# Linear attention and two MLPs on one core: kv products in halves of the array's columns, four units' q exponentials by ScalarE, v queued ahead of the first weights

## Chip, cores and metric

The kernel runs on one core of a Trainium2 chip. The metric is device time in microseconds of one execution; smaller is better. Engines are named as the profile names them: PE (TensorE matmul), PEld (TensorE weight load), DVE (VectorE), ACT (ScalarE), POOL (GpSimd) and SP (SyncE, which here only issues DMAs).

## The reference

```python
# q, k, v: 8 batches x 8 heads x 576 tokens x 64, float32
q_s = softmax(q, over the 64 features)
k_s = softmax(k, over the 576 tokens)
kv  = einsum('bhsd,bhse->bhde', k_s, v)      # 64 x 64 for each head
y   = einsum('bhsd,bhde->bhse', q_s, kv)     # -> 4608 tokens x 512
h   = y @ w_in1;  y = leaky_relu(h, 0.01) @ w_out1       # 512 -> 2048 -> 512
h   = y @ w_in2;  y = silu(h) @ w_out2                   # 512 -> 2048 -> 512
```

The softmaxes subtract the maximum and divide by the sum plus 1e-9.

## The kernel before

**Units.** Attention is cut into 36 units. Unit n is a block j of 512 output tokens (9 blocks) and a pair p of heads (4 pairs), so units 0 to 3 are block 0, units 4 to 7 are block 1, and so on. For n below 32 a unit also makes the kv of one batch and one pair of heads, so there are 32 kv products. Three generators make a unit: `k_task` (softmax of k and the kv product), `v_task` (loads of v) and `q_task` (softmax of q, transposes, and the product with kv that gives x, the operand of the first MLP layer).

**The kv product (L507 to L509).** The 576 tokens are four chunks of 128 and a rest of 64. The stationary operand is a chunk of exp(k), 128 tokens by 128 features of two heads. The moving operand is v of both heads with a column of ones behind it, 129 columns, so that the last column of the result is the sum of the softmax. The fifth matmul takes the 64 tokens of the rest, and so 64 rows of the array. Only the two diagonal 64 x 64 blocks of the result are kept: L515 and L516 make the reciprocal of the sum on DVE, and L521 copies the two blocks, scaled, into `kv` on ACT. All of it is float32, and the trace shows each float32 matmul as two instructions.

**The softmax of q (L571 to L603).** DVE takes the negated maximum (L572). For units below `NS` = 8 the maximum is subtracted in one instruction (L577), ACT takes one exponential of 512 columns (L581), and DVE sums it (L583). For later units ACT takes eight exponentials of 64 columns, each with the maximum as its bias and with a sum of its own (L592). Then DVE adds the epsilon and inverts (L598, L599), and L601 multiplies.

**The order of work.** A small planner, `Queues`, runs when the program is built. Every generator yields its next operation with an estimated cost (`op(("A", 0.4))` for ACT, `"D"` for a DMA of SP, `"p"` and `"P"` for PE), and the planner emits the one that can start first on the estimated clock. Among those that could start together the smaller rank goes first. The emitted order is the program order of each engine, and SP's order is the order of all DMAs. In `v_task` each of the three loads is planned only when the one before it has landed by the estimate. At n below 4 the ranks are r = -40 + 5n for k, r + 1 for q, r + 5 for v; the weights of the first layer (`split1(f)`, L350) have rank -36 + 6f for f below 4.

**The rest.** The first layer (`layer0`, L651 to L653) multiplies x by w_in1 as three float32r products. Its weights are decoded by DVE and ACT (`decode`, L329 to L346, then L296 and L292). It runs blocks 0 and 1 in parts, f below 6 first, and attention of the later blocks runs in between. The other three layers (L872, L922) follow, with a Strassen-like scheme on seven products. L691 stores the activations of the first layer to DRAM.

Of the kernel before, what the change touches and what calls it, by code (L numbers as in the profile page):

```python
# [13 lines left out]
ACTF = mybir.ActivationFunctionType  # L14
# [48 lines left out]
class Queues:  # L63
# [14 lines left out]
    def spawn(self, rank, gen):  # L78
        self.tasks.append([rank, next(self.count), self.now, gen, None, 0.0, None])
        self.tasks.sort(key=lambda t: t[:2])  # L80
        self.step(next(t for t in self.tasks if t[3] is gen), None)
# [121 lines left out]
def linear_attention_two_mlps(  # L203
# [24 lines left out]
    nc = tc.nc  # L228
    B, H, S, D = q.shape
    NT, DM = out.shape  # L230
    DFF = w_in1.shape[1]
    P = 128
    TB = 512
    NB = NT // TB
    NP = H // 2
# [3 lines left out]
    SR = S - SM  # L239
    EPS = 1e-9  # L240
    FS = 6
    NU = 8
    NS = 8
# [18 lines left out]
    gd = [tc.dram_tile([NG, 4, P, TB], F32, name=f"gd{j}") for j in range(NB)]  # L262

    NKV = 8
    NV = 2 * D + 1
    ident = const.tile([P, P], F32, name="ident")
    ones = const.tile([P, 1], F32, name="ones")
    kvbuf = [const.tile([P, P], F32, name=f"kv{i}") for i in range(NKV)]
# [7 lines left out]
    done, spawn = qs.done, qs.spawn  # L276
# [158 lines left out]
    sets = []  # L435
# [5 lines left out]
    for n in range(3):  # L441
        t = gp.tile([P, 2, TB], F32, tag=f"g{n}", name=f"uq{n}")
        r_q.add(t[:, 0], t[:, 1])

    def k_task(n):

        b, j, p = units[n]
        if n >= NU:
            yield wait(("kvs", n - NU))
        of[n] = yield get(r_kv)  # L450
        kf, vv = of[n]
        done(("set", n))
        heads = slice(2 * p, 2 * p + 2)

        yield op(("D", 0.73))
        nc.sync.dma_start(
            out=kf[:, 0:512].rearrange("p (h c) -> p h c", h=2),
            in_=k[b, heads, 0:SM, :].rearrange("h (p c) d -> p h (c d)", c=4),
        )
        kh = kf[:, 0:512].rearrange("p (h c d) -> p h c d", c=4, h=2)  # L460
        k4 = kf[:, 0:512].rearrange("p (h c d) -> p c h d", c=4, h=2)
        yield op(("D", 0.56))
        k1 = kf[0:SR, 512:640]
        nc.sync.dma_start(
            out=k1.rearrange("p (h d) -> p h d", h=2), in_=k[b, heads, SM:S, :].rearrange("h p d -> p h d")
        )
        m1 = yield get(r_m)
        m2 = yield get(r_o)
        m2v = m2[:, 0:4 * D].rearrange("p (h c d) -> p h c d", h=2, c=2)
        yield op(("V", v_tt(256)))  # L470
        nc.vector.tensor_tensor(out=m2v, in0=kh[:, :, 0:2], in1=kh[:, :, 2:4], op=ALU.max)
        yield op(("V", v_tt(128)))
        nc.vector.tensor_tensor(out=m1, in0=m2v[:, :, 0], in1=m2v[:, :, 1], op=ALU.max)
        r_o.put(m2)
        m1f = m1.rearrange("p h d -> p (h d)")
        yield op(("V", v_tt(128)))
        nc.vector.tensor_tensor(out=m1f[0:SR], in0=m1f[0:SR], in1=k1, op=ALU.max)
        pm = yield get(r_attn)
        yield op(("p", 0.12))
        nc.tensor.transpose(pm[:, 0:P], m1f, ident)  # L480
        r_m.put(m1)
        nm = small[n % NU]["k"][:, 0:1]
        yield op(("V", v_tt(128)))
        nc.vector.tensor_reduce(out=nm, in_=pm[:, 0:P], axis=AX.X, op=ALU.max, negate=True)
        yield op(("p", 0.12))
        nc.tensor.transpose(pm[:, P:2 * P], nm.to_broadcast([P, P]), ident)
        nb = pm[:, P:2 * P]
        yield op(("V", v_tt(512)))
        nc.vector.tensor_tensor(
            out=k4, in0=k4,  # L490
            in1=nb.rearrange("p (h d) -> p h d", h=2).unsqueeze(1).to_broadcast([P, 4, 2, D]), op=ALU.add,
        )
        yield op(("V", v_tt(128)))
        nc.vector.tensor_tensor(out=k1, in0=k1, in1=nb[0:SR], op=ALU.add)
        r_attn.put(pm)
        kx = yield get(r_kx)
        yield op(("A", a_(512)))
        nc.scalar.activation(
            out=kx.rearrange("p (c h d) -> p c h d", c=4, h=2), in_=k4, func=ACTF.Exp
        )  # L500
        yield op(("A", a_(128)))
        nc.scalar.activation(out=k1, in_=k1, func=ACTF.Exp)
        yield wait(("v", n), *([("xm", n - NKV + NP)] if n >= NKV - NP else []))
        vv = vv.rearrange("p (c n) -> p c n", c=5)
        pk = yield get(r_attn)
        yield op(("p", 1.1))
        for c in range(4):  # L507
            nc.tensor.matmul(pk[:, 0:NV], lhsT=kx[:, c * P:(c + 1) * P], rhs=vv[:, c, :], start=c == 0, stop=False)  # L508
        nc.tensor.matmul(pk[:, 0:NV], lhsT=k1, rhs=vv[0:SR, 4, :], start=False, stop=True)  # L509
        r_kv.put(of.pop(n))  # L510
        r_kx.put(kx)
        done(("kv", n))
        rk = small[n % NU]["k"][:, 1:2]
        yield op(("V", 0.15))
        nc.vector.tensor_scalar_add(rk, pk[:, 2 * D:NV], EPS)  # L515
        nc.vector.reciprocal(out=rk, in_=rk)  # L516
        w = kvbuf[(b * NP + p) % NKV]
        for i in range(2):
            o = slice(i * D, (i + 1) * D)
            yield op(("A", a_(64)))  # L520
            nc.scalar.activation(out=w[o, o], in_=pk[o, o], func=ACTF.Copy, scale=rk[o])  # L521
        kv[b, p] = w
        r_attn.put(pk)
        done(("kvs", n))

    def v_task(n):
        b, j, p = units[n]
        yield wait(("set", n))
        t = of[n][1]
        t = t.rearrange("p (c n) -> p c n", c=5)  # L530
        for i in range(2):
            yield op(("D", 0.73))
            nc.sync.dma_start(
                out=t[:, 0:4, i * D:(i + 1) * D],
                in_=v[b, 2 * p + i, 0:SM, :].rearrange("(p c) d -> p c d", c=4),
            )

            yield wait()
        yield op(("D", 0.56))
        nc.sync.dma_start(  # L540
            out=t[0:SR, 4, 0:2 * D].rearrange("p (h d) -> p h d", h=2),
            in_=v[b, 2 * p:2 * p + 2, SM:S, :].rearrange("h p d -> p h d"),
        )
        yield wait()
        done(("v", n))
# [9 lines left out]
    def q_task(n):  # L555

        b, j, p = units[n]
# [14 lines left out]
        nc.vector.tensor_reduce(out=nq, in_=qv, axis=AX.X, op=ALU.max, negate=True)  # L572
        sq = rq = small[n % NU]["rq"]
        x4 = qx.rearrange("p (c h d) -> p c h d", c=4, h=2)
        if n < NS:
            e = yield op(("G", 1.0), ("V", v_tt(512)))
            engines[e].tensor_tensor(  # L577
                out=qv, in0=qv, in1=nq.unsqueeze(2).to_broadcast([P, 8, D]), op=ALU.add
            )
            yield op(("A", a_(512)))  # L580
            nc.scalar.activation(out=x4, in_=q4, func=ACTF.Exp)  # L581
            yield op(("V", v_tt(512)))
            nc.vector.tensor_reduce(  # L583
                out=sq, in_=qx.rearrange("p (a d) -> p a d", a=8), axis=AX.X, op=ALU.add
            )
        else:

            for c in range(4):
                for h in range(2):
                    at, to = 4 * h + c, 2 * c + h  # L590
                    yield op(("A", 0.4))
                    nc.scalar.activation(  # L592
                        out=x4[:, c, h], in_=q4[:, c, h], func=ACTF.Exp, bias=nq[:, at:at + 1],
                        accum_out=sq[:, to:to + 1],
                    )
# [379 lines left out]
    with tc.manual_schedule():  # L975
        nc.vector.memset(ones, 1.0)
        make_identity(nc, ident)
        nc.scalar.activation(out=small[0]["k"][:, 0:1], in_=ones, func=ACTF.Exp)
        for _, t in sets:
            nc.gpsimd.memset(t.rearrange("p (c n) -> p c n", c=5)[:, :, 2 * D:], 1.0)  # L980
        for t in kvbuf:
            nc.gpsimd.memset(t, 0.0)

        for n in range(NP):
            r = -40 + 5 * n
            spawn(r, k_task(n))
            spawn(r + 1, q_task(n))
            spawn(r + 5, v_task(n))
        for n in range(NP, len(units)):
            b, j, p = units[n]  # L990
            r = -12 + 3 * p if j == 1 else step(j, 0) - 14 + 4 * p
            if b is not None:
                spawn(r, k_task(n))
                spawn(r, v_task(n))
            spawn(r, q_task(n))
        for f in range(NF):
            spawn(-36 + 6 * f if f < 4 else step(0, f) - 4, split1(f))
            if f < NH:
                spawn(f, layer0(0, f))
        spawn(0, layer0_all())  # L1000
        for t in (convert1, convert2, convert3):
            spawn(1000, t())
        spawn(0, later())
        for i in range(NG):
            for l in (1, 2, 3):
                spawn(step2(l, 0, i) - 8, weights(l, i))
        spawn(step2(1, 0, 0) - 4, g_all(1))
        spawn(step2(2, 0, 0) - 5, x_all())
        spawn(step2(3, 0, 0) - 4, g_all(3))
        spawn(step2(1, 0, 0), layers())  # L1010
        qs.run()
# [30 lines left out]
```

## Time and profile before

| | us |
|---|---|
| median of 3 runs (1629.92 to 1631.63) | 1631.16 |
| the profiled execution | 1635.08 |
| its span, first to last instruction | 1633.1 |
| PE busy | 1603.1 |
| DVE busy | 1194.2 |
| ACT busy | 851.3 |
| POOL busy | 39.1 |

PE is busy in 98% of the span. Busy PE is not PE at its peak: instructions overlap, so what a matmul costs is read from the distance between starts and not from its duration. Times on the left of a timeline row are microseconds from the start of the span.

### The profile page before, as it was taken

Reading aid. Unit: us, or ns where it says so; the run is one execution under the profiler, and the core shown is the slowest. Engines: PE = TensorE matmul, PEld = TensorE weight load, DVE = VectorE, ACT = ScalarE, POOL = GpSimd, SP = SyncE. Lnnn points to the kernel's source line nnn. Section 1 sums busy time; section 2 is a strip of 40 time slices with the busy share of each in tenths; the row PEclk is TensorE's granted clock in tenths of the full one; section 3 lists DMA queues with packets and bytes.
Section 4 is the critical chain, followed back from the end, with each engine's and each line's share of the span. In section 5 each row is a group of like instructions: output and inputs, shape, how many; then the busy total and the mean of one; then the engine's idle time right before and its main releaser. Section 6 shows DMA issues by size and latency. Waiting matters only on the chain.

```text
span 1633.1 us, 30896 instructions
## 1 busy us (share of the span) xinstructions
PE 1603.1 (98%) x11456; PEld 1501.8 (92%) x11456; DVE 1194.2 (73%) x2205; ACT 851.3 (52%) x1824; POOL 39.1 (2%) x53
## 2 busy tenths in 40 slices
PE   6899999999999999999999999999999999999999
PEld 4688888888788999999999999999999999999999
DVE  8886656657566887777788966666669877777775
ACT  5768756766445544444447433444446544444442
POOL 2101001000000000000000000000000000000000
PEclk9899999999999999999999999999999999999999
DMA  8766767777779655454558344333338544444442
GB/s 227 234 195 167 209 196 240 212 242 230 225 235 311 214 150 168 141 170 145 166 143 277 131 152 140 131 133 133 135 130 279 163 131 135 133 130 136 134 132 78
DMA packets 251030, 287.25 MB, mean 176 GB/s; under 512 B 59392, under 2 KB 182272, under 8 KB 250880
## 3 DMA queue, kind: packets, MB, share of 16 engines
q1 hardware_dynamic: 250880, 285.29, 56.6%
q8 instruction: 90, 1.47, 0.4%
q14 instruction: 60, 0.49, 0.1%
HBM read 168.82 MB, written 116.39 MB: 175 GB/s over the span
## 4 chain that ended last, share of the span: by engine, by line
PE 93%; DVE 5%; DMA 1%; issue 0%; ACT 0%; SPq 0%; DVEq 0%; ACTq 0%
PE b L922 22%; PE h L922 21%; PE b L872 11%; PE h L872 11%; PE h L651 8%; PE h L653 8%; PE h L652 8%; PE a L623 2%; PE a L508 2%; PE a L608 1%; DVE o L810 1%; PE a L509 1%; DVE a L292 1%; DVE x L292 1%; DVE g L292 0%
## 5 line engine op out<-in xcount | busy, mean ns | idle before, releaser
L651 PE MATMUL h<-x,w 128*128 128x512 f32 x576 | 238.5, 414 | 2.3 <-ACT w L296 1.6
L296 ACT ACTIVATE x<-x 128x512 fp32r<-128x512 f32 x209 | 131.8, 631 | 205.8 <-DMA x<-gda 91.0
L653 PE MATMUL h<-x,w 128*128 128x512 f32 x576 | 225.9, 392 | 1.2 <-DVE w L292 1.2
L652 PE MATMUL h<-x,w 128*128 128x512 f32 x576 | 225.4, 391 | 0.8 <-DVE x L292 0.5
L810 DVE TENSOR_TENSOR o<-o,b 128x512 f32<-128x512 f32 x190 | 128.1, 685 | 72.5 <-PE b L872 39.7
L810 DVE TENSOR_TENSOR o<-o,h 128x512 f32<-128x512 f32 x188 | 126.6, 685 | 62.7 <-PE h L872 36.7
L884 ACT ACTIVATE o<-o 128x512 f32<-128x512 f32 x144 | 89.2, 629 | 145.5 <-DVE o L810 144.7
L684 ACT ACTIVATE o<-h 128x512 f32<-128x512 f32 x144 | 85.9, 597 | 118.0 <-PE h L653 109.0
L296 ACT ACTIVATE x<-o 128x512 fp32r<-128x512 f32 x169 | 105.2, 631 | 70.0 <-DVE o L810 53.8
L922 PE MATMUL b<-a,x 128*128 128x256 f32 x1080 | 141.4, 283 | 0.1
L292 DVE TENSOR_TENSOR x<-x 128x512 fp32r<-128x512 f32 x209 | 137.2, 684 | 2.5
L651 PEld LDWEIGHTS h<-x,w 128*128 128x128 f32 x576 | 108.8, 189 | 29.2 <-ACT w L296 2.5
L922 PEld LDWEIGHTS b<-a,x 128*128 128x128 f32 x1080 | 134.7, 192 | 0.3 <-DVE x L292 0.3
L922 PE MATMUL b<-x,a 128*128 128x256 f32 x1044 | 132.0, 284 | 0.6 <-DVE x L292 0.5
L653 PEld LDWEIGHTS h<-x,w 128*128 128x128 f32 x576 | 108.4, 188 | 25.6 <-DVE w L292 2.3
L872 PE MATMUL h<-x,a 128*128 128x256 f32 x1008 | 130.0, 283 | 1.3 <-DVE x L292 1.3
L652 PEld LDWEIGHTS h<-x,w 128*128 128x128 f32 x576 | 108.9, 189 | 22.8 <-issue 1.2
L922 PEld LDWEIGHTS b<-x,a 128*128 128x128 f32 x1044 | 128.1, 192 | 1.1 <-DVE x L292 1.0
L872 PEld LDWEIGHTS h<-x,a 128*128 128x128 f32 x1008 | 124.9, 192 | 1.5 <-DVE x L292 1.5
L922 PE MATMUL h<-x,a 128*128 128x256 f32 x996 | 126.0, 283 | 0.2
L872 PE MATMUL b<-x,a 128*128 128x256 f32 x960 | 123.8, 283 | 1.3 <-DVE x L292 1.3
L922 PEld LDWEIGHTS h<-x,a 128*128 128x128 f32 x996 | 122.3, 192 | 0.7 <-DVE x L292 0.6
(116 smaller groups left out, 2819.3 us busy)
## 6 DMA issues: line engine op xcount, KB each, us to landing
gda<-o SPq DMA_DIRECT2D x144, 256.0 KB, 2.6
gd<-o SPq DMA_DIRECT2D x144, 256.0 KB, 2.6
x<-gd SPq DMA_DIRECT2D x102, 256.0 KB, 2.7
x<-gda SPq DMA_DIRECT2D x89, 256.0 KB, 2.8
a<-wc SPq DMA_DIRECT2D x84, 256.0 KB, 4.3
wc<-o SPq DMA_DIRECT2D x72, 256.0 KB, 3.2
raw<-in_moe_w_out_dram SPq DMA_DIRECT2D x32, 512.0 KB, 4.2
g<-gda SPq DMA_DIRECT2D x37, 256.0 KB, 2.7
```

Of the source, the lines that this page charges most:

```text
L292: engines[e].tensor_tensor(out=out_, in0=a, in1=b.bitcast(F32), op=ALU.subtract)
L296: nc.scalar.activation(out=out_, in_=in_, func=ACTF.Copy)
L508: nc.tensor.matmul(pk[:, 0:NV], lhsT=kx[:, c * P:(c + 1) * P], rhs=vv[:, c, :], start=c == 0, stop=False)
L623: nc.tensor.matmul(po, lhsT=kv[bb, p], rhs=qT.rearrange("p (c t) -> p c t", c=4)[:, :, a:e], start=True, stop=True)
L651: nc.tensor.matmul(h, lhsT=w[:, 0, kk], rhs=x[:, 0], start=kk == 0, stop=False)
L652: nc.tensor.matmul(h, lhsT=w[:, 0, kk], rhs=x[:, 1], start=False, stop=False)
L653: nc.tensor.matmul(h, lhsT=w[:, 1, kk], rhs=x[:, 0], start=False, stop=kk == KD - 1)
L684: nc.scalar.activation(out=o, in_=h, func=ACTF.Prelu, alpha=0.01)
L810: nc.vector.tensor_tensor(out=o, in0=a, in1=b, op=alu)
L872: nc.tensor.matmul(bank[:, r * HB:(r + 1) * HB], lhsT=w4[:, a, r, k], rhs=x3[:, b, k], start=n == 0, stop=n == 5,)
L884: nc.scalar.activation(out=t, in_=t, func=ACTF.Silu)
L922: nc.tensor.matmul(bank[:, m * HB:(m + 1) * HB], lhsT=s[:, a, at:at + P], rhs=x[:, b, r * HB:(r + 1) * HB], start=i + m + n == 0, stop=i = ...
```

## The change

The kv product is made per head. For each of five chunks and each of two heads one matmul has as stationary operand the chunk's 64 columns of that head, as moving operand the head's 64 columns of v with a column of ones behind them (65 columns), and writes its half of the partitions of the result. The rest of 64 tokens is now a chunk of 128 like the others, whose lower half is zeros in k and in v; POOL writes the zeros and the ones once, at the start, into the six sets of buffers. For units 0 to 3 the softmax of q takes the branch with eight exponentials. The rank of `v_task` for these units becomes r + 2.

```diff
-    NV = 2 * D + 1
+    NV = 2 * (D + 1)
...
-        for c in range(4):
-            nc.tensor.matmul(pk[:, 0:NV], lhsT=kx[:, c * P:(c + 1) * P], rhs=vv[:, c, :], start=c == 0, stop=False)
-        nc.tensor.matmul(pk[:, 0:NV], lhsT=k1, rhs=vv[0:SR, 4, :], start=False, stop=True)
+
+        for c in range(5):
+            kc = kx[:, c * P:(c + 1) * P] if c < 4 else kf[:, 512:640]
+            for h in range(2):
+                o = slice(h * D, (h + 1) * D)
+                nc.tensor.matmul(
+                    pk[o, 0:D + 1], lhsT=kc[:, o], rhs=vv[:, c, h * (D + 1):(h + 1) * (D + 1)],
+                    start=c == 0, stop=c == 4,
+                )
...
-        nc.vector.tensor_scalar_add(rk, pk[:, 2 * D:NV], EPS)
+        nc.vector.tensor_scalar_add(rk, pk[:, D:D + 1], EPS)
...
-            nc.scalar.activation(out=w[o, o], in_=pk[o, o], func=ACTF.Copy, scale=rk[o])
+            nc.scalar.activation(out=w[o, o], in_=pk[o, 0:D], func=ACTF.Copy, scale=rk[o])
...
-                out=t[:, 0:4, i * D:(i + 1) * D],
+                out=t[:, 0:4, i * (D + 1):i * (D + 1) + D],
...
-            out=t[0:SR, 4, 0:2 * D].rearrange("p (h d) -> p h d", h=2),
+            out=t[0:SR, 4].rearrange("p (h d) -> p h d", h=2)[:, :, 0:D],
...
-        if n < NS:
+        if NP <= n < NS:
...
-        for _, t in sets:
-            nc.gpsimd.memset(t.rearrange("p (c n) -> p c n", c=5)[:, :, 2 * D:], 1.0)
+        for t_, t in sets:
+            t5 = t.rearrange("p (c h d) -> p c h d", c=5, h=2)
+            nc.gpsimd.memset(t5[:, :, :, D:], 1.0)
+
+            nc.gpsimd.memset(t_[SR:P, 512:640], 0.0)
+            nc.gpsimd.memset(t5[SR:P, 4, :, 0:D], 0.0)
...
-            spawn(r + 5, v_task(n))
+            spawn(r + 2, v_task(n))
```

## Rows read from the trace of the kernel before

**Rows 1.** Windows, all engines: busy us (instructions), PEclk, DMA share, GB/s.

```profile
12.00:24.00 12.00, 8.54 (x30) 6.49 (x29) 10.56 (x23) 7.31 (x14) 3.12 (x3) 1.00 0.93 262
24.00:36.00 12.00, 10.13 (x48) 6.75 (x48) 11.45 (x27) 7.08 (x16) 3.40 (x3) 1.00 0.74 197
46.00:68.00 22.00, 17.93 (x79) 12.27 (x77) 17.86 (x51) 16.63 (x39) 6.47 (x6) 0.78 0.93 290
110.00:361.00 251.00, 251.00 (x1255) 205.89 (x1254) 160.38 (x434) 178.85 (x620) 15.88 (x15) 1.00 0.69 208
```

**Rows 2.** Timeline of PE around one kv product: start us, us, instruction.

```profile
111.48 0.39 PE L653 MATMUL h<-x,w 128*128 128x512 f32 x1
111.71 1.05 PE L508 MATMUL a<-u,kx 128*128 128x129 f32 x8
...
112.70 0.49 PE L509 MATMUL a<-u,u 64*128 64x129 f32 x2
113.11 0.50 PE L651 MATMUL h<-x,w 128*128 128x512 f32 x1
113.45 0.39 PE L652 MATMUL h<-x,w 128*128 128x512 f32 x1
```

**Rows 3.** The same stretch: the last L508 alone, then a weight load (PEld).

```profile
112.49 0.27 PE L508 MATMUL a<-u,kx 128*128 128x129 f32 x1
...
113.11 0.19 PEld L651 LDWEIGHTS h<-x,w 128*128 128x128 f32 x1
```

**Rows 4.** Windows of line L508 alone: PE busy (instructions), PEld busy.

```profile
110.00:365.00 255.00, 25.45 (x192) 24.14 (x192) 1.00 0.69 208
```

**Rows 5.** Timeline of DVE and POOL: the softmax of q of unit 1.

```profile
12.88 0.67 DVE L572 TENSOR_REDUCE q<-uq 128x8 f32<-128x512 f32 x1
...
13.63 1.04 POOL L577 TENSOR_TENSOR uq<-uq,q 128x512 f32<-128x512 f32 x1 [2.80 <-DVE q L572]
...
16.98 0.17 DVE L598 TENSOR_SCALAR rq<-rq 128x8 f32<-128x8 f32 x1
```

**Rows 6.** Timeline of DVE: the sum of unit 3, and what follows it back to back.

```profile
32.66 0.67 DVE L583 TENSOR_REDUCE rq<-o 128x8 f32<-128x512 f32 x1
33.25 0.67 DVE L292 TENSOR_TENSOR x<-a,x 128x512 fp32r<-128x512 f32 x1
```

**Rows 7.** Timeline of ACT: one exponential of 512, then exponentials of 64 with sums.

```profile
22.98 0.61 ACT L296 ACTIVATE w<-o 128x512 fp32r<-128x512 f32 x1
23.50 0.61 ACT L581 ACTIVATE o<-uq 128x512 f32<-128x512 f32 x1
...
104.32 0.34 ACT L592 ACTIVATE o<-uq,q 128x64 f32<-128x64 f32 x1
104.65 0.34 ACT L592 ACTIVATE o<-uq,q 128x64 f32<-128x64 f32 x1
```

**Rows 8.** Timeline of SP and POOL at the start, and PE's first kv product.

```profile
1.44 1.19 POOL L982 MEMSET kv<- 128x128 f32 x8
...
2.64 0.47 SPq L319 DMA_DIRECT2D rw<-in_moe_w_in_dram  x1
3.15 0.58 SPq L533 DMA_DIRECT2D u<-in_v_dram  x1
...
9.79 1.04 POOL L601 TENSOR_TENSOR o<-o,rq 128x512 f32<-128x512 f32 x1 [2.84 <-DVE rq L599]
...
10.97 0.62 SPq L540 DMA_DIRECT2D u<-in_v_dram  x1
...
14.08 1.93 PE L508 MATMUL a<-u,kx 128*128 128x129 f32 x8
```

**Rows 9.** The chain that ended last, a kv product in it: start us, us, what.

```profile
52.30 1.83 PE a L508 x8
54.13 0.73 PE a L509 x2
...
67.43 0.64 ACT w L296
```

## The prediction

> **What bounds the kernel now.** I read the page first: PE is busy in 98% of the span and holds nearly all of the chain that ended last, so the end moves only with what PE must do and with the time in which it has nothing to do. The windows by stage [rows 1] then split the span in two. From 110 to 361 us, where the attention of the later blocks runs between matmuls of the first layer, PE is busy in 251.00 of 251 us, DVE in 160 and ACT in 179. There the engines that feed PE have room, and a microsecond that PE saves is a microsecond of the end. Before 68 us PE waits. DVE is busy in 10.56 of 12 us and in 11.45 of 12 us, the DMA engines at 0.93 in the first of these windows, ACT in only 7.3 and 7.1. From 46 to 68 us PE's clock is at 0.78 on average, and the first matmul of the steady stretch starts only behind the decoded weights that ACT writes at 67.43 [rows 9]. There the end moves with DVE, SP's order and ACT. The change touches both: its kv part works on the first stretch, its q and v parts on the second.
>
> **What one kv product costs PE now.** The timeline of PE is read by starts [rows 2, 3]. The eight instructions of L508 start between 111.71 and 112.49, so 0.78 / 7 = 0.111 us apart, and the two of L509 should follow at that pace: ten times 0.111 is 1.11 us. But L509 starts at 112.70 where 112.60 was due, 0.10 late. The L652 behind the product starts at 113.45. An undisturbed matmul of the first layer takes 0.23 (L653 at 111.48, the next start at 111.71), so the product ended in effect at 113.45 - 0.23 = 113.22, which is 0.30 behind 112.70 + 2 x 0.111 = 112.92. The product costs 1.51 us: 1.11 of streaming, 0.40 for entering and leaving the 64-row shape. The weight load of the L651 behind it starts at 113.11, with its matmul and not ahead of it, which is part of those 0.30.
>
> **What it costs after.** Five chunks by two heads by two instructions make 20 instructions of 65 columns in place of 10 of 129. The 64-row shape is gone, but the array is now entered and left in halves of its columns. The trace holds no such shape. I take the same 0.40, as the nearest change of shape; the bounds are 0 (no price) and 0.80 (twice). The streaming is the open term. Half as many columns is 0.0555 us for an instruction, if it goes with the columns. If the two halves then run wholly beside each other, the 20 take 10 x 0.0555 = 0.56 us. If they don't, 20 x 0.0555 = 1.11, as now. If an instruction does not get shorter at all (bounded by its weight load or its issue), 20 x 0.111 = 2.22. The row that it is nearest to is L508, whose pitch holds a load and a matmul at once: the loads do run under matmuls here, PEld is busy in 206 of the 251 us in which PE is never idle [rows 1], and nothing in it speaks for a half-width load as long as a whole one. Between whole overlap and none I take the middle, 0.83 us: twice as many instructions must pass the same sequencer, so I do not expect the whole factor. The product then costs 0.83 + 0.40 = 1.23, which saves 0.28 us.
>
> The count: L508 has 192 instructions from 110 us on [rows 4], so 24 of the 32 products stand where PE is the bound. 24 x 0.28 = 6.7 us saved; 24 x 0.55 = 13.2 with whole overlap, 0 with none, and 24 x 1.11 = 26.6 lost at the other end. The other eight stand where PE waits anyway. Of these, one on the chain runs at the 1.2 GHz level (1.83 us for 8 is 0.229 each, twice 0.111) and takes 2.56 [rows 9]. Scaled by 1.23 / 1.51 it saves 0.5.
>
> The Trainium skill speaks against overlap at one place: "TensorE: Matmul & The Clock Gate", Part 3, says that a weight load overlaps a running matmul only when the row group differs, and the two column halves have the same rows. By it the loads of the 20 instructions would stand between the matmuls, and the product would lengthen towards the 2.22 above. The trace already disagrees for the whole array, whose loads share all rows and still hide [rows 1], so I give that case little. "TensorEngine Tiling (Array Packing)", Key Properties, says the opposite, that tiles load and multiply in parallel; no run before shows it.
>
> **q of units 0 to 3.** Three instructions change. POOL loses L577, 1.04 us a unit [rows 5]; POOL is idle most of the time, so only the latency counts. DVE loses L583, which holds it 0.59 (starts at 32.66 and 33.25) [rows 6]: 4 x 0.59 = 2.4 us. ACT loses one exponential of 0.52 (22.98 to 23.50 is the pitch of such instructions) and gains eight of 0.33 (104.32 to 104.65, with the read of the accumulator inside) [rows 7]: 2.64 - 0.52 = 2.1 us a unit, 8.5 in all. ACT was busy in 14.4 of the 24 us from 12 to 36 [rows 1]; with three units' share there, 6.4, it is at 20.8 of 24: full, but not the bound. The path itself gets no longer: from the maximum to the epsilon takes 16.98 - 12.88 = 4.1 us now, through three engines [rows 5], and eight exponentials after a maximum of 0.67 are 3.3. What queues behind the eight on ACT are the exponentials of k and the copies that x needs; a copy that comes late by up to 0.33 holds up its x. DVE was nearly full from 12 to 36 us, and the weights that PE waits for at 68 us are decoded on it, so I take DVE's 2.4 us as gained. Bounds: 4 lost (ACT's 8.5 less what its 9.6 idle us in these windows can't take at the right time, about half) and 4 gained (DVE's 2.4, and PE's clock not falling).
>
> **v, and the fills.** By the ranks, v of unit 0 passes the first weights and nothing else: unit 1's v already stood ahead of unit 2's k by the order in which they are spawned, and the others stay behind the same loads. SP issues the weights at 2.64 and the first piece of v at 3.15 [rows 8]; they swap, so v is 0.5 earlier and the weights 0.6 later. PE's first kv product starts at 14.08, 3.1 us behind the issue of the last piece of v at 10.97, so it may come up to 1.5 earlier by the planned chain of three loads; the first decode comes 0.6 later. I take 0, bounds 1.5 gained and 0.6 lost. The ones and zeros are 18 fills in place of 6. By the 1.19 / 8 = 0.15 of the fills of kv, 12 more are 1.8 us, and POOL is done at 2.63 + 1.8 = 4.4. Its next work now is L601 at about 9.8 [rows 8], so they cost nothing; if a load of k had to wait for them it would cost under 1 us.
>
> **Sum.** Against the profiled execution, 1635.08: - 6.7 (24 products) - 0.5 (one at the start) - 2.4 (DVE) = 1625.5. The median of the runs stands 3.92 below the profiled execution, so 1621.6. About 0.2%, 3.3 us, is what a measurement of this kernel tells from no change.
>
> **Rivals.**
> - *Whole overlap.* The halves run wholly beside each other: 1631.2 - 13.2 - 2.9 = 1615. For it: each half has its own columns and its own weights. Against: 40 instructions (loads and matmuls) in 0.56 us.
> - *The halves don't overlap.* The product stays at 1.51, and only the start gains: 1631.2 - 2.4 = 1629, no change that can be told. For it: instructions of PE start in order, and the trace has never two matmuls side by side.
> - *A half costs as much as a whole (slower).* 2.22 + 0.40 per product: 1631.2 + 26.6 - 2.4 = 1655. Its place is the 24 products from 110 us on, and it decides against the change as soon as one of the 20 instructions takes over 0.0555 us plus 2.4 / 480 = 0.0605 us. For it: all weight loads in the trace take about 0.19 us whatever their rows; against: they overlap.
> - *ACT is crowded at the start.* The kv part saves its 6.7, but x of units 0 to 3 comes late, the bound of 4 us is lost: 1631.2 - 6.7 + 4 = 1628.5. For it: ACT's order is fixed, and it would have 3 of 24 us to spare. Against: the shorter path of q.
>
> **Chances and range.** Partial overlap, my forecast, 0.36; whole overlap 0.20; none 0.22; a half as dear as a whole 0.12; ACT crowded 0.10. The likeliest one's own range is 1617 to 1626. From 1610 (whole overlap and a cheaper change of shape) to 1634 (none, and the start's small losses) the range leaves out the dear half and little else. Faster by over 0.2% are the first two, a third of "none" and half of the last: 0.67. Same: 0.18. Slower: 0.15.
>
> **What would show it.** In the steady stretch, the starts of the product's 20 instructions and of the L652 behind it: under 1.51 from the first to the effective end is right, and two halves with the same start show overlap. PE must stay without idle time from 110 us on; if it waits there, the saving stops at that wait. At the start: L583 four times in place of eight, ACT under 11 of 12 us from 12 to 36, the first steady L651 at about 65 in place of 68 us. The forecast is wrong if the pitch of the halves is above 0.0555 without overlap, or if the start of the steady stretch moves by more than 4 us either way, most of all by PE's clock falling at another place.

## Result, and the profile after

| | before | after |
|---|---|---|
| median of 4 runs, us | 1630.54 (1629.75 to 1631.63) | 1611.09 (1610.54 to 1611.78) |
| ratio | | 0.9874 (0.9856 to 0.9892) |
| profiled execution, us | 1635.08 | 1610.83 |
| its span, us | 1633.1 | 1609.0 |

The change saves 19.5 us where 9.5 were forecast. The time lies inside the stated range, near its lower end; the size was off by a factor of two. On the four chips of the experiments below the kernel before had medians from 1631.9 to 1633.7 over 9 to 17 runs, with single runs from 1629.6 to 1636.4; the changed kernel ran on one of them at 1611.95 (1611.26 to 1612.26).

Where did it go? First, the stages. Windows of the changed kernel, columns as in [rows 1]:

```profile
12.00:24.00 12.00, 9.12 (x59) 5.31 (x58) 11.35 (x28) 10.00 (x38) 2.03 (x2) 1.00 1.05 281
24.00:36.00 12.00, 9.62 (x84) 5.93 (x84) 11.47 (x29) 10.92 (x39) 3.45 (x3) 1.00 0.72 181
46.00:68.00 22.00, 17.03 (x125) 12.14 (x124) 21.59 (x55) 20.00 (x45) 5.32 (x5) 1.00 1.02 317
110.00:361.00 251.00, 251.00 (x1522) 203.53 (x1521) 167.53 (x443) 189.71 (x651) 19.48 (x17) 1.00 0.74 229
```

PE still has no idle time from 110 us on, so what a product saves there arrives at the end. From 46 to 68 us DVE is busy in 21.59 of 22 us, where it had 17.86 [rows 1], and PE's clock is at 1.00, where it had 0.78.

Now one kv product, beside [rows 2]. It stands at 26 us, at a clock of 1.00. In the changed kernel's trace the products from 103 us on keep its distances: from the first L512 to whatever comes next it is 0.73 us each time (two products stand back to back and take 1.32). In the kernel before the same distance is 1.40 (111.71 to 113.11). Timeline of PE, then of its weight loads:

```profile
26.07 0.39 PE L659 MATMUL h<-x,w 128*128 128x512 f32 x1
26.39 0.69 PE L512 MATMUL a<-u,kx 128*64 128x65 f32 x16
26.91 0.29 PE L512 MATMUL a<-u,u 128*64 128x65 f32 x4
27.12 0.50 PE L657 MATMUL h<-x,w 128*128 128x512 f32 x1
27.46 0.39 PE L658 MATMUL h<-x,w 128*128 128x512 f32 x1
```

```profile
26.39 0.55 PEld L512 LDWEIGHTS a<-u,kx 128*64 128x64 f32 x16 [0.36 <-issue]
26.85 0.20 PEld L512 LDWEIGHTS a<-u,u 128*64 128x64 f32 x4
```

It is read as in the prediction. The first sixteen instructions take 26.91 - 26.39 = 0.52, so 0.0325 us each on average, and twenty take 0.65. The product was due at 26.07 + 0.23 = 26.30 and starts at 26.39, 0.09 late. It ended in effect at 27.46 - 0.23 = 27.23, which is 0.19 behind 26.39 + 0.65 = 27.04. So 0.65 + 0.28 = 0.93 us in place of 1.51, and 24 x 0.58 = 13.9 us of the gain. The sixteen loads end within 0.55 us: they run under the matmuls.

Do two halves start together? Two narrow windows of the same rows, 26.45 to 26.48 and 26.50 to 26.54, count what has started and still runs:

```profile
26.39 0.28 PE L512 MATMUL a<-u,kx 128*64 128x65 f32 x2
26.39 0.34 PE L512 MATMUL a<-u,kx 128*64 128x65 f32 x4
```

By 26.48 two have started. Each of them lasts 0.27 us and the two together 0.28, so they start within 0.01 us of each other. By 26.54 there are four. In the trace this goes on: ten pairs, each within 0.01 us; the second pair stands 0.11 behind the first, and each later one 0.058 behind the one before it. Ten pairs at 0.058 are 0.58 us. So the halves overlap wholly, and the other 0.35 of the 0.93 are spent once for a product: 0.09 before it, 0.05 between its first two pairs, and 0.2 behind it.

The rest is the start. The steady stretch begins with the first L651 (L657 after the change) that waits for the decoded weights of ACT; before, that was at 68.11, behind the weights of [rows 9].

```profile
60.15 0.50 PE L657 MATMUL h<-x,w 128*128 128x512 f32 x1 [1.07 <-ACT w L296]
```

It is 8.0 us earlier. Both profiled executions together: 13.9 + 8.0 = 21.9 of the 24.1 us between their spans. Most of the other 2 us is a low clock behind that point: the kernel before began its steady stretch at a clock of 0.84 from 68 to 80 us, the changed one at 1.00, and 0.16 x 12 is 1.9 us. The runs' medians lie 19.5 apart, because the profiled execution of the kernel before, at 1635.08, was among its longer ones.

### The profile page after: what moved, and what is told of

Its sections match the earlier page's. It is cut to its first block, busy times and chain, and to the rows that moved or that the text cites. A ratio compares the mean times of both kernels' runs of the same rounds, so it can differ in the third digit from the quotient of the medians.

```text
span 1609.0 us, 31572 instructions
## 1 busy us (share of the span) xinstructions
PE 1577.6 (98%) x11776; PEld 1477.0 (92%) x11776; DVE 1190.3 (74%) x2199; ACT 858.7 (53%) x1884; POOL 39.7 (2%) x63
## 3 DMA queue, kind: packets, MB, share of 16 engines
q8 instruction: 92, 1.51, 0.4%
## 4 chain that ended last, share of the span: by engine, by line
PE 92%; DVE 4%; DMA 2%; SPq 1%; issue 1%; ACT 0%; POOL 0%; DVEq 0%; POOLq 0%; ACTq 0%
PE b L928 22%; PE h L928 21%; PE b L878 11%; PE h L878 11%; PE h L657 8%; PE h L659 8%; PE h L658 8%; PE a L629 2%; PE a L512 1%; PE a L614 1%; DVE x L292 1%; DVE a L292 1%; DMA a<-wc 1%; DVE o L816 1%; DMA u<-in_k_dram 0%
## 5 line engine op out<-in xcount | busy, mean ns | idle before, releaser
L657 PE MATMUL h<-x,w 128*128 128x512 f32 x576 | 237.1, 412 | 1.8 <-ACT w L296 1.1
L292 DVE TENSOR_TENSOR x<-x 128x512 fp32r<-128x512 f32 x209 | 137.2, 684 | 2.5
L657 PEld LDWEIGHTS h<-x,w 128*128 128x128 f32 x576 | 108.5, 188 | 28.0 <-ACT x L637 1.8
L659 PEld LDWEIGHTS h<-x,w 128*128 128x128 f32 x576 | 108.1, 188 | 24.1 <-DVE w L292 0.8
```

The costliest lines, as they stand in the source:

```text
L292: engines[e].tensor_tensor(out=out_, in0=a, in1=b.bitcast(F32), op=ALU.subtract)
L657: nc.tensor.matmul(h, lhsT=w[:, 0, kk], rhs=x[:, 0], start=kk == 0, stop=False)
L659: nc.tensor.matmul(h, lhsT=w[:, 1, kk], rhs=x[:, 0], start=False, stop=kk == KD - 1)
```

## Experiments

All ratios are against the kernel before, run on the same chip in the same job. "Steady start" is the start of that first L651 in the profiled execution (in q_only and kv_q it follows without a wait).

| kernel | median us | ratio | steady start us |
|---|---|---|---|
| kv part alone (kv_only) | 1617.31 | 0.9895 (0.9882 to 0.9909) | 65.33 |
| q part alone (q_only) | 1628.52 | 0.9969 (0.9957 to 0.9980) | 63.25 |
| v part alone (v_only) | 1628.35 | 0.9967 (0.9955 to 0.9979) | 63.66 |
| kv and q (kv_q) | 1613.51 | 0.9888 (0.9874 to 0.9902) | 62.52 |
| kv and v (kv_v) | 1613.34 | 0.9888 (0.9871 to 0.9904) | 63.14 |
| all three (after_again) | 1611.95 | 0.9871 (0.9853 to 0.9889) | 60.98 |
| heads one behind the other (heads_apart) | 1622.65 | 0.9930 (0.9918 to 0.9943) | 61.29 |
| zeros, whole width (zeros_full) | 1625.20 | 0.9959 (0.9946 to 0.9972) | 66.37 |

**The parts, alone and in pairs.** Each kernel takes the diff's hunks of its parts and leaves the others.

> This is the kernel before with the kv part of the change alone (matmuls in halves, zeros and ones filled in); the softmax of q and the rank of v as before. Theory: the 24 products in the stretch where PE never waits cost 0.93 us in place of 1.51, so 24 x 0.58 = 13.9 us of the gain of 19.5 are theirs: ratio about 0.9915 (1616.6 us). Rival, that the gain stands mostly at the start: ratio 0.996 or more.

> This is the kernel before with only the softmax of q of units 0 to 3 on the eight exponentials with sums. Theory: DVE loses four sums of 0.59 us and four stretches of about 0.75 us in which a POOL instruction held up a DVE instruction, 5.4 us in all, and the start of the steady stretch moves by that: ratio about 0.9967. Rival A, that only the four sums count: 2.4 us, ratio 0.9985. Rival B, that ACT is crowded: ratio 1.000 or above.

> This is the kernel before with only the rank of the loads of v of units 0 to 3 changed. Theory: one swap in SP's order, worth nothing that can be told: ratio within 0.999 to 1.001. Rival: v lands earlier and the first kv products with it, 1.5 us gained: ratio 0.999 or less.

> This is the changed kernel with the old rank of v. Theory, that the start is bound by DVE and POOL: v's rank is worth under 1 us beside the other two parts, ratio 0.988. Rival, that v's rank is worth alone what it gave alone (5.3 us): ratio 0.991.

> This is the changed kernel with the old softmax of q for units 0 to 3. Theory, that DVE and POOL bind the start: 3 to 5 us are lost, ratio 0.990. Rival, that the start gains once, by PE's clock not falling, whichever part brings it: ratio 0.9875, as with all three.

> The changed kernel on this chip, for comparison: ratio 0.9874, 1611 us.

The kv part alone reaches 0.9895, beyond the 0.9915 of its 24 products: its early products shorten the start too (steady start 2.8 us earlier). The q part gives 0.9969, the value of the first theory and not of its rivals; but a part of that value is luck, as the runs by clock below show. The v part gives 0.9967, where its theory had expected nothing and its rival 1.5 us. Together the parts give less than their sum, since the start can gain only once: beside kv, the q part takes 1617.3 to 1613.5 and the v part to 1613.3, each about 4 us, and the second of the two adds 1.4 to 2.4. These differences are of medians on different chips, whose fastest runs of the kernel before lie within 0.3 us of each other; by the ratios the step from kv_only is only 1.1 us, inside the intervals. kv_q came between its theory's 0.988 and its rival's 0.991; kv_v at 0.9888 between 0.9875 and 0.990.

**Do the halves run beside each other?** The kernel changed, with its two loops exchanged:

```diff
-        for c in range(5):
-            kc = kx[:, c * P:(c + 1) * P] if c < 4 else kf[:, 512:640]
-            for h in range(2):
+        for h in range(2):
+            for c in range(5):
+                kc = kx[:, c * P:(c + 1) * P] if c < 4 else kf[:, 512:640]
```

> This is the changed kernel with the two loops of the kv product exchanged: all five chunks of the first head, then all five of the second, so neighbours in the order use the same half of the columns (but for one pair). Theory, that the halves run beside each other: without a neighbour in the other half the 20 instructions start 0.0555 us apart in place of 0.0325, a product costs 0.46 us more, 24 products 11 us: ratio about 0.9943 against the kernel before. Rival, that a half instruction is simply that short: the pitch stays 0.0325 and the ratio at 0.9875.

Timeline of PE around one product of heads_apart (L480 is a transpose behind the product; the three dots stand for three instructions):

```profile
105.83 0.40 PE L659 MATMUL h<-x,w 128*128 128x512 f32 x1
106.16 0.73 PE L512 MATMUL a<-u,kx 128*64 128x65 f32 x10
...
106.79 0.45 PE L512 MATMUL a<-u,kx 128*64 128x65 f32 x5
107.08 0.28 PE L512 MATMUL a<-u,u 128*64 128x65 f32 x2
107.29 0.33 PE L480 MATMUL a<-ident,m 128*128 128x128 f32 x1
```

From the first of the twenty instructions to the transpose behind them it is 107.29 - 106.16 = 1.13 us. One half alone starts an instruction every (107.08 - 106.79) / 5 = 0.058 us, the distance of the pairs in the changed kernel. So an instruction is as short as there; it only has no neighbour. (Not quite: at the seam three of the second head start beside the last of the first. The row of ten shows it, since the program has eight of them ahead of the first head's last two.) In the changed kernel the same distance, from the first L512 to an L480 behind it, is 0.74:

```profile
103.44 0.69 PE L512 MATMUL a<-u,kx 128*64 128x65 f32 x16
103.96 0.29 PE L512 MATMUL a<-u,u 128*64 128x65 f32 x4
104.18 0.33 PE L480 MATMUL a<-ident,m 128*128 128x128 f32 x1
```

24 x (1.13 - 0.74) = 9.4 us; the medians differ by 1622.65 - 1611.95 = 10.7. The steady start is 0.3 us later than in after_again, and behind it, from 62 to 68 us, heads_apart has PE's clock at 0.72 where after_again has 1.00, which is 0.28 x 6 = 1.7 us. The theory holds, its rival falls: neighbours in different halves overlap, and that is worth 9 of the products' 24 x 1.13 = 27 us.

**What is the 64-row shape worth?** The kernel before with its fifth matmul filled up to 128 rows, the products in the whole width:

```diff
-        nc.tensor.matmul(pk[:, 0:NV], lhsT=k1, rhs=vv[0:SR, 4, :], start=False, stop=True)
+        nc.tensor.matmul(pk[:, 0:NV], lhsT=kf[:, 512:640], rhs=vv[:, 4, :], start=False, stop=True)
...
+            nc.gpsimd.memset(t_[SR:P, 512:640], 0.0)
+            nc.gpsimd.memset(t5[SR:P, 4, 0:2 * D], 0.0)
```

> This is the kernel before with only the rest of 64 tokens filled up with zeros to 128 rows; the products stay 128 columns wide with 129 moving columns, ten instructions. Theory: the 0.40 us for entering and leaving the 64-row shape goes, the streaming of 1.11 stays; 24 x 0.40 = 9.6 us, ratio about 0.994. Rival, that the price belongs to the change of operands from float32 to float32r and not to the shape: ratio 1.000.

```profile
122.26 0.40 PE L653 MATMUL h<-x,w 128*128 128x512 f32 x1
122.49 1.06 PE L508 MATMUL a<-u,kx 128*128 128x129 f32 x8
123.39 0.39 PE L509 MATMUL a<-u,u 128*128 128x129 f32 x2
123.53 0.47 PE L651 MATMUL h<-x,w 128*128 128x512 f32 x1
123.84 0.40 PE L652 MATMUL h<-x,w 128*128 128x512 f32 x1
```

L509 follows at the pace of L508 and the product ends in effect at 123.84 - 0.23 = 123.61: 1.12 us. The whole 0.40 is gone, so it belongs to the shape. By the trace that is 24 x 0.39 = 9.4 us; the medians show 7.2, and 9.4 (0.9942) lies just outside the interval. The runs by clock below close the gap: all five of zeros_full have a mean granted clock of 0.996 to 0.998, and the kernel before takes 1634.9 at 0.995 to 0.997, 9.7 more. So of the 13.9 us two thirds come from filling up the rows, and the halves bring the other 4.5: 0.46 us less streaming a product, against 0.28 for their own change of shape.

**What bounds the start?** Two kernels add to the changed one what the q part took away, in work that nothing reads and without the planner's knowledge, so that all other instructions keep their order: two adds on 256 columns on POOL behind the maximum (pool_side), and the sum of 512 columns on DVE (dve_side), both for units 0 to 3.

```diff
+        for i in range(2 if n < NP else 0):
+            nc.gpsimd.tensor_tensor(
+                out=idle, in0=idle, in1=nq[:, 4 * i:4 * i + 4].unsqueeze(2).to_broadcast([P, 4, D]), op=ALU.add
+            )
```

```diff
+        if n < NP:
+            nc.vector.tensor_reduce(
+                out=idle, in_=ident.unsqueeze(1).to_broadcast([P, 4, P]), axis=AX.X, op=ALU.add
+            )
```

> This is the changed kernel with two more POOL adds on 256 columns that nothing reads, behind the maximum of q in each of units 0 to 3; the order of all other instructions is that of the changed kernel. The output does not change. Theory, that POOL holds up DVE: DVE instructions beside them last about 0.7 us longer, four times, and the end comes 2 to 4 us later than in after_again. Rival, that POOL's work is hidden: within 1 us of after_again.

> This is the changed kernel with four more sums on DVE (512 columns, 0.59 us each) that nothing reads, where the sums of q of units 0 to 3 stood before; the order of all other instructions is that of the changed kernel. The output does not change. Theory, that DVE is the bound at the start: 2.4 us later than after_again. Rival, that DVE's idle time takes them: within 1 us of after_again.

Each of the two also clears its extra tile once on DVE, at the start (0.27 and 0.06 us). pool_side ran at 1613.80, dve_side at 1613.81, both 1.9 us behind after_again. For each kernel one window of DVE, from 0 to the steady start (busy us, instructions, PEclk, DMA share, GB/s): first the kernel before, then the changed one, after_again, pool_side, dve_side.

```profile
0.00:68.11 68.11, 56.22 (x139) 0.93 0.80 233
```

```profile
0.00:60.15 60.15, 51.43 (x131) 1.00 0.88 243
```

```profile
0.00:60.98 60.98, 51.50 (x131) 1.00 0.87 241
```

```profile
0.00:62.37 62.37, 52.64 (x132) 0.97 0.83 234
```

```profile
0.00:62.76 62.76, 53.77 (x136) 0.97 0.88 232
```

Subtract the rows. dve_side does 53.77 - 51.50 = 2.27 us more on DVE and starts its steady stretch 1.78 later, with 0.5 less idle time: DVE is the bound, nearly one for one. pool_side does 1.14 more on DVE, 0.27 of it for clearing the tile, and starts 1.39 later. And the change itself: 56.22 - 51.43 = 4.8 us less work on DVE ahead of the steady start, and 11.89 - 8.72 = 3.2 less idle time, together the 8.0 us. What DVE no longer waits for is seen in its waits up to the steady start (us in total, times, longest), of the kernel before and of the changed one:

```profile
DVE k L515 <- PE a L509: 3.4, 3, 1.9
```

```profile
DVE k L484 <- PE a L480: 0.2, 1, 0.2
```

DVE's order is fixed: L515 waits for the kv product, and everything behind it on DVE waits too. The product is shorter after the change, and no wait for it is left in the list. But not all of the 3.4 us is the product's length. In before_ten, further down, the products are the old ones and the clock holds until 64 us, and these waits are 1.6 us; in kv_q the products are the new ones and the clock falls (0.53 from 54 to 62 us), and they are 2.0. The low clock makes a part of them. Against the gain stands a longer wait for the loads of k (L471): 4.8 us after the change, 2.7 before.

That a POOL instruction can hold up DVE is seen in the durations. Timeline of the changed kernel, POOL and DVE (L335 is the same instruction of two tiles):

```profile
11.75 1.23 POOL L607 TENSOR_TENSOR o<-o,rq 128x512 f32<-128x512 f32 x1 [5.79 <-DVE k L484]
12.12 1.15 DVE L335 TENSOR_SCALAR o<-o 128x512 uint32<-128x512 uint32 x1
...
21.73 0.41 DVE L335 TENSOR_SCALAR o<-o 128x512 uint32<-128x512 uint32 x1
```

L335 takes 1.15 us beside a POOL instruction and 0.41 without. The Trainium skill, "SBUF — State Buffer", section "SBUF: two separate sides", says that a GpSimd instruction and certain VectorE instructions take a shared pair of ports for their whole length and that the other one blocks; the trace agrees, with 0.74 us for this one. But it doesn't explain the gain. Summed over the DVE instructions up to 68 us that exceed the shortest of their line and shape by over 0.25 us, the excess is 7.5 us in the kernel before, 3.9 in q_only and again 7.0 in the changed kernel: there are fewer POOL instructions there, but as much stretching. In pool_side the sum is 7.1, so its 1.9 us are not this stretching. What else they are was not separated: its adds also stand ahead of POOL's own multiplications, which start 0.5 us later than in after_again (12.83 for 12.33, 19.93 for 19.39).

An earlier pair had the same two aims but told the planner of the extra work, which moved the order of everything behind it. pool_add is pool_side with a planned cost of 0.55 for each add:

```diff
+            for i in range(2 if n < NP else 0):
+                yield op(("G", 0.55))
+                nc.gpsimd.tensor_tensor(
...
```

> This is the changed kernel with eight more POOL instructions: after the maximum of q of each of units 0 to 3, two adds on a tile of 256 columns that nothing reads, in the place where the subtraction of 512 columns stood before. They do not change the output. Theory, that POOL holds up DVE: each pair stretches DVE instructions by about 0.7 us, 3 us in all, and the steady stretch starts up to 3 us later: ratio up to 0.9893. Rival, that POOL's work is hidden: ratio 0.9875, and no DVE instruction longer than in the changed kernel.

It took 1616.21, ratio 0.9907 (0.9893 to 0.9921), beyond its theory's 0.9893 and 2.4 us more than pool_side with the same work on another chip. That difference I put down to the planner's order.

**Moving more off POOL and DVE.** mult_dve puts the multiplication of the first eight units on DVE, q_all_act puts units 4 to 7 on the eight exponentials too:

```diff
-        e = yield op(("G", 1.0), ("V", v_tt(512)))
+        e = yield op(*([("G", 1.0)] if n >= NU else []), ("V", v_tt(512)))
```

```diff
-        if NP <= n < NS:
+        if False:
```

> This is the changed kernel with the multiplication by the reciprocal (512 columns) of the first eight units on DVE in place of POOL. Theory, that a POOL instruction of 1.04 us holds up DVE by about 0.7 us while the same work on DVE takes 0.59: eight times 0.1 to 0.7 us gained, 1 to 4 us, ratio 0.985 to 0.987. Rival, that DVE is the bound and POOL's work comes free: 8 x 0.59 = 4.7 us lost, ratio 0.990.

> This is the changed kernel with units 4 to 7 on the eight exponentials with sums as well. Theory, that DVE is the bound from 36 to 60 us: four more sums of 0.59 and four more POOL instructions fall away, 3 to 5 us gained, ratio 0.985. Rival, that ACT, busy in 20 of 22 us from 46 to 68 in the changed kernel, becomes the bound: 4 x 2.1 = 8.5 us more work on it, 0 to 4 us lost, ratio 0.9875 to 0.990.

mult_dve took 1614.97, ratio 0.9892 (0.9875 to 0.9909): the rival's side, 3.0 us behind after_again where the rival had 4.7. Its clock also fell (0.71 from 54 to 62 us), so the 3.0 are not DVE's time alone. q_all_act took 1616.97, ratio 0.9909 (0.9893 to 0.9924), 5.0 us behind after_again and so a little past the 0 to 4 of its rival. Its window from 46 to 68 us (columns as in [rows 1]) shows DVE at 13.21 of 22 us, where the changed kernel has 21.59, and PE's clock at 0.70:

```profile
46.00:68.00 22.00, 14.38 (x94) 8.70 (x88) 13.21 (x39) 19.35 (x69) 2.29 (x2) 0.70 0.93 290
```

Up to its steady start DVE waits 5.1 us for copies of x by ACT (L292 behind L637), a wait that the changed kernel's list does not have. So four units on ACT is the best number here, of 0, 4 and 8.

**PE's clock.** The kernel before has PE at the 1.2 GHz level in parts of 50 to 58 and 62 to 72 us, behind waits; the changed kernel doesn't. before_warm and kv_q_warm plan filler matmuls into PE's gaps, before_ten puts ten into the kernel before without the planner:

```diff
+    def warm():
+        yield wait(("unit", 3))
+        n = 0
+        while ("w", 4) not in qs.events:
+            bank = yield get(r_attn)
+            yield op(("P", 0.22))
+            nc.tensor.matmul(bank[:, 0:P], lhsT=ident, rhs=ident, start=True, stop=True)
+            r_attn.put(bank)
+            n += 1
```

```diff
         nc.tensor.transpose(pm[:, 0:P], m1f, ident)
+        for _ in range(6 if n == 6 else 0):
+            nc.tensor.matmul(pm[:, 2 * P:3 * P], lhsT=ident, rhs=ident, start=True, stop=True)
...
         nc.tensor.transpose(pm[:, P:2 * P], nm.to_broadcast([P, P]), ident)
+        for _ in range(4 if n == 6 else 0):
+            nc.tensor.matmul(pm[:, 2 * P:3 * P], lhsT=ident, rhs=ident, start=True, stop=True)
```

> This is the kernel before with 27 float32 matmuls of the identity, 0.22 us each, that nothing reads, planned into PE's gaps between the end of unit 3 and the decoding of the fifth tile of weights. They do not change the output. Theory, that the kernel before loses some 3 to 5 us at the start to PE's clock falling to 1.2 GHz after idle stretches: with PE kept busy the clock holds and the ratio is about 0.998. Rival, that the clock's fall is hidden under waits for DVE and DMA: the ratio is 1.000 or, as the fillers stand in the way of the products, up to 1.003, with or without the lower clock.

> This is the changed kernel with the old rank of v and with fillers as in before_warm in PE's gaps. With the old rank of v the changed kernel took 1613.5 us and showed the lower clock from 54 to 66 us. Theory, that the rank of v helped the changed kernel through the clock: with the fillers the clock holds and the time is about 1611, ratio 0.9875. Rival, that v's earlier landing itself counts: 1613.5 or more, ratio 0.9888.

> This is the kernel before with ten float32 matmuls of the identity (0.22 us each) that nothing reads, six and four of them in the two stretches between 48.7 and 51.6 us in which PE waited, ahead of the fall of its clock; the order of all other instructions is that of the kernel before. The output does not change. Theory, that the clock's fall costs the kernel before: the clock holds from 50 to 58 us, the products there end up to 3 us earlier, and the time is 1.5 to 4 us under the kernel before, with a smaller spread of the runs. Rival, that the waits for DVE and SP cover it: within 1 us of the kernel before.

The planned fillers tell nothing of the clock: it holds (1.00 throughout), but before_warm took 1636.07, ratio 1.0020 (1.0010 to 1.0030), and kv_q_warm 1620.52, 7.0 above kv_q, because the order moved and fillers stood ahead of products, as here in before_warm:

```profile
63.65 3.12 PE L973 MATMUL a<-ident 128*128 128x128 f32 x12
66.61 1.06 PE L508 MATMUL a<-u,kx 128*128 128x129 f32 x8
```

before_ten is cleaner. Its clock holds from 50 to 58 us, DVE does the same work up to the steady start (56.45 us) and waits 2.4 less, 9.5 in place of 11.9:

```profile
0.00:65.97 65.97, 56.45 (x139) 1.00 0.83 238
```

But PE then waited for weights for 2.08 us, and the clock fell there: the next matmuls start 0.43 us apart.

```profile
65.97 0.80 PE L655 MATMUL h<-x,w 128*128 128x512 f32 x1 [2.08 <-ACT w L296]
66.56 0.63 PE L656 MATMUL h<-x,w 128*128 128x512 f32 x1
66.99 0.63 PE L657 MATMUL h<-x,w 128*128 128x512 f32 x1
```

The median was 1632.65 beside 1632.49, ratio 0.9999 (0.9989 to 1.0008): the rival's result. The runs lie closer together (11 of 12 from 1631.3 to 1633.2, where the kernel before has 17 from 1629.6 to 1635.8).

The recorded runs say more when they are put in order by their mean granted clock. In the profiled execution of the kernel before, at 0.995, PE is at the 1.2 GHz level from 51.3 to 58.1 and from 64.9 to 71.8 us. One such stretch lowers the mean of the span by about 0.002. The 55 runs of the kernel before on the four chips:

| mean granted clock | runs | median us | lowest to highest |
|---|---|---|---|
| 1.000 | 19 | 1630.2 | 1629.6 to 1631.2 |
| 0.998 or 0.999 | 13 | 1632.2 | 1630.5 to 1633.3 |
| 0.995 to 0.997 | 23 | 1634.9 | 1633.8 to 1636.4 |

So the kernel before comes with no fall, with about one or with two, and a median over all depends on how many of each it holds. All eight runs of the changed kernel have 1.000. Against the first row it gains some 18 to 19 us: 13.9 for the products and 4 to 5 at the start, with the clock held on both sides; against the last row the gain is nearly 5 us more. The q and the v part alone (clock 0.999 or 1.000 in all runs) lie 1.7 and 1.8 us below the first row, where their ratios make it 5.2 and 5.3. This is an order among runs and no experiment: which of the two, the waits or the clock, comes first in a long run isn't shown by it.

## Why the prediction was wrong

- **The bound, right.** PE had no idle time from 110 us on, before and after, and the 24 products are worth what the trace shows. The start is bound by DVE; dve_side shows it nearly one for one.
- **The overlap of the halves, wrong.** The step "between whole overlap and none I take the middle, 0.83 us" is the first that failed, and with it its reason, that twice as many instructions must pass the same sequencer. The halves start in pairs within 0.01 us of each other: whole overlap, the rival that was given 0.20. That rival's product, 0.56 + 0.40 = 0.96 us, is near the 0.93 measured, and its 13.2 us for 24 products near the 13.9. Counted from the average distance, the streaming took 0.65 and not 0.83.
- **The change of shape, mis-sized.** "I take the same 0.40" measured 0.28 by that count, 0.09 going in and 0.19 coming out. Together with the streaming: 0.58 saved where 0.28 stood, 13.9 us where 6.7 stood. This is 7.2 of the 10 us by which the sum was short.
- **The other rivals of the product.** Half instructions as dear as whole ones are far off: 0.058 us against 0.111. So is the rule of the Trainium skill weighed there ("TensorE: Matmul & The Clock Gate", Part 3): loads of two halves with the same rows ran under the matmuls. What "TensorEngine Tiling (Array Packing)", Key Properties, of the Trainium skill says of tiles loading and multiplying in parallel agrees with the pairs. Two readings behind these rivals were off: the loads of transposes take 0.14 us and not 0.19, and in the kernel before a transpose and the L651 behind it often start 0.02 to 0.03 us apart, so matmuls side by side were not unknown there.
- **q, mis-sized.** "I take DVE's 2.4 us as gained" gave 4 us as the second part, beside kv, and 1.4 to 2.3 as the last. The four sums count nearly in full (dve_side, 1.9). Alone, against runs of the kernel before that held the clock, the part is worth 1.7, so the 2.4 was no bad size for DVE's share; the rest, PE's clock not falling, stood only in its bound of 4. That "POOL is idle most of the time, so only the latency counts" is in doubt: pool_side costs 1.9 us, and whether POOL's latency or something else carries them is open.
- **v, wrong.** "They swap" and "I take 0" failed: the part gives 4 us as the second, beside kv, and 1.6 to 2.4 as the last. The swap also brings unit 0's second and third pieces ahead, the last from 10.97 to 9.61 us in the changed kernel (9.85 in v_only). That did not bring the first kv product forward: it starts at 14.08 before, at 14.09 after and at 14.24 in v_only. But the planner, whose estimated clock this moves, then orders all later work otherwise. With it DVE does 53.57 us of work up to the steady start in v_only, where it was 56.22, and in its profile PE's clock is at 1.00 throughout. That it was the new order that brought this was not tested by itself.
- **The start as a sum.** I priced each edit by its own engine, 2.9 us in all. The steady start moved by 8.0 us in the profiles, beyond the 4 us that the prediction named as a sign against it. What binds is DVE's work and DVE's waits in one fixed order: 3.4 us of waits at L515 went, by the shorter product and by the clock that held, and the 0.5 us for "one on the chain" did not hold them. The profile before was moreover one of the long runs, with two falls of the clock, and the sum set out from it.
- **ACT crowded, not here.** ACT was at 20.9 of 24 us from 12 to 36, as worked out (20.8), and the q part still gained. With eight units (q_all_act) the rival comes true.
- **Open.** What makes the clock fall in one run of the kernel before and not in the next, and how the start's 4 to 5 us at a held clock divide among the three parts. The runs of the kernel before at 1.000 held the clock of themselves, but none of them was profiled.

## What to carry to other kernels

A lone matmul on half of the array's rows can cost more for the change of shape (0.40 us) than for its streaming (0.22); filling it up with zeros bought 9 of 14 us here, before any halves. Issue the two column halves alternately: one head behind the other lost the overlap. In a start whose order is fixed, count the work and the waits of the engine that is full up to the first steady instruction, and test a cost with work that the planner doesn't see, since a planned one moves everything behind it. Where runs differ in their mean granted clock, compare those that have the same.

## Not expected of the hardware

- Twenty instructions of 65 columns in float32 started in pairs, 0.058 us from pair to pair, in alternating column halves, and singly, 0.058 apart, in one half at a time, weight loads included.
- With one half behind the other, the second half's first instruction started ahead of the first half's last three, which stand before it in the program.
- Entering and leaving the shape of two column halves cost 0.09 and 0.19 us beside the average distance of the instructions; that of 64 rows 0.10 and 0.30.
- A DVE instruction with one input in SBUF (L335) lasted 1.15 us beside a POOL instruction and 0.41 alone.
